# The first pair's down product as seven block products in a second last stage

## The chip, the cores and the metric

The kernel runs on one core of a Trainium2 chip. The metric is device time in microseconds (us) of that core for one launch; the time shown is the median of three runs. Besides the timed runs there is one profiled execution with its trace. Engines: PE (TensorE matmul; its weight loads are listed as PEld), DVE (VectorE), ACT (ScalarE), POOL (GpSimd) and SP (SyncE), which here issues all DMAs.

## The reference

Inputs are float32; S = 2048 tokens, D = 512, F = 1376, 32 heads of 16. The block is a linear attention and a bilinear FFN, each behind a layernorm with a modulation from `c`:

```
mod = silu(c) @ w_mod ; sa, ba, ga, sf, bf, gb = split(mod, 6)
x = A_x + ga * linear_attention(layernorm(A_x) * (1 + sa) + ba)
n = layernorm(x) * (1 + sf) + bf
h = (n @ w_gate) * (n @ w_up)            # 2048 x 1376
out = x + gb * (h @ w_down)              # 2048 x 512
```

The change is in the last line, for half of the tokens and eight elevenths of F. A product of two float32 matrices is made on PE from a high and a low part of each operand (type fp32r): high by high, high by low, low by high, three matmuls for one.

## The kernel before

The tokens are four chunks of 512, each four token tiles of 128; F is eleven f tiles: 0 to 9 of 128 columns and 10 of 96. Chunks 0 and 1 are the first pair, 2 and 3 the second. Attention and the layernorms of the first pair come first. For the first pair f tiles 8, 9 and 10 are done whole, gate, up and down (`gate_up`, lines L958 to L986), beside the attention of the others.

The rest of the FFN is the generator `ffn()`. Its steps each make one f tile's gate and up products for one pair of chunks at once, as a product of 2x2 blocks with seven products in place of eight (`block`; the products are `times`, L1158, 6 matmuls of 512 columns each, 42 a step). The seven follow in the order a11 b11, s1 t1, s2 t2, a12 b21, s3 t3, s4 b22, a22 t4: letters a and s are blocks of the tokens' side and their sums (tile name `h`), b and t blocks of the weights and their differences (tile name `w`). Side work hangs on named points of a step: p1, p5, p6, p2, p7, p3 and p4 stand behind the seven products in that order. The table `plan`, with keys (step, point), and the lists given to `gates` say what is done there. Steps 0 to 7 are the first pair's, with f = 0 to 7; steps 8 to 18 the second pair's.

The weights of a step are a `Right`: four raw loads of 128 KB (L1096), sums on POOL (L1102), high parts on ACT (L1113, L1116), low parts on POOL (L1120). In the first pair's steps the seven tiles of a right are also stored to DRAM (`park`, L1135, seven DMAs of 256 KB), and the second pair's steps fetch them from there (`Fetched`, L1147). The tokens' side of the second pair is made during the first pair's steps; 14 of its tiles are stored (`aside`, L1068) and 14 fetched (`fetch`, L1083) at the end of step 7, since there is no room for both sides. The stows (L1002) are parts of the second pair's normalized tokens on their way through DRAM.

The down product of the first pair is `down_group` (L1241 to L1243). After each second step it takes the two f tiles just made, multiplies their h tiles by rows of w_down (scaled by gb on DVE, split on ACT and POOL), for two chunks of four token tiles, with 24 matmuls of 512 columns at a place (eight such places, cut by `parts` so that they lie between steps), and DVE adds the sums to x (`evac`, L945). So h tiles are used up soon after they are made. The down product of the second pair is the class `Down`: its h tiles stay in the tile pool, five pairs of f tiles (8,9), (0,1), (2,3), (4,5), (6,7) each give 2x2 blocks, tile 10 goes along as an odd one, and after the last step `run` makes seven products, each over the five pairs and partly the odd tile. A product into one pair of PSUM banks uses `mm` (L1455, three matmuls of 256 columns per pair and token tile), one into four banks `mm_wide` (L1463 and L1464, one of 512 and one of 256). The combinations of w_down for it are made during the second pair's steps, stored (L1393) and fetched in the last stage (L1400). The last products' sums are added to x and stored (L1525, L1528).

What sets the order: each engine runs its instructions in program order. All DMAs are issued by SP, in order, and at most eight are outstanding: a DMA waits for the eighth before it. A tile pool of 94 buffers and eight PSUM banks (four named `bank`, four `acc`) limit what can be in flight.

## Time and profile before

| what | value |
|---|---|
| time, median of 3 runs | 540.4 us (539.95 to 540.65) |
| the profiled execution's own time | 539.58 us |
| its span | 537.9 us |
| granted TensorE clock | 1.00 |
| PE busy | 532.6 us, 99% of the span |
| DVE, ACT, POOL busy | 408.1, 297.7, 160.0 us |
| moved by DMA | 109.21 MB, mean 203 GB/s |

The span runs from the first to the last instruction; the time is some 1.7 us more than the span. A busy time is the sum over an engine's instructions without idle time between them. In the trace the first pair's steps run from about 250 to 363 us, the second pair's from 363 to 478.9, and the second pair's down product from there to the end.

### The profile page before, as it was taken

What the parts mean: (1) busy time and instruction counts of PE and PEld (TensorE: products, weight loads), DVE (VectorE), ACT (ScalarE), POOL (GpSimd) and SP (SyncE); (2) the same over time, 40 slices, a digit from 0 to 9 for tenths busy, and PEclk for the clock granted to TensorE, in tenths of its full rate; (3) what the DMA queues carried; (4) which work ended last, traced back from release to release, by engine and by line L of the source; (5) the groups of instructions that cost most, each with busy time, mean ns of one, the idle gap of its engine ahead of it and who ended that gap; (6) DMA issues with size and microseconds to landing.
All of it is one profiled execution on the core that took longest, in us unless ns stands there. A gap on an engine that the chain in (4) does not pass through costs nothing.

```text
span 537.9 us, 8026 instructions
## 1 busy us (share of the span) xinstructions
PE 532.6 (99%) x2549; PEld 444.7 (83%) x2549; DVE 408.1 (76%) x701; ACT 297.7 (55%) x564; POOL 160.0 (30%) x170
## 2 busy tenths in 40 slices
PE   8999999999999999999999999999999999999997
PEld 7888888888888878878888888887888888889997
DVE  7997879999989888779766576996556564669772
ACT  3696877648587765577684545454434334246030
POOL 2001010010021220076696577747532322210000
PEclk9999999999999999999999999999999999999999
DMA  8902427310165165947869596794289998689222
GB/s 283 387 35 92 144 98 216 98 60 2 45 195 194 41 209 147 310 143 228 279 197 319 207 323 224 216 372 120 74 300 334 388 389 315 229 278 392 83 77 81
DMA packets 86396, 109.21 MB, mean 203 GB/s; under 512 B 10897, under 2 KB 41617, under 8 KB 86353
## 3 DMA queue, kind: packets, MB, share of 16 engines
q1 hardware_dynamic: 86352, 108.70, 60.3%
q8 instruction: 20, 0.33, 0.3%
q14 instruction: 24, 0.19, 0.1%
HBM read 65.93 MB, written 42.73 MB: 202 GB/s over the span
## 4 chain that ended last, share of the span: by engine, by line
PE 99%; DVE 0%; issue 0%
PE bank L1158 27%; PE acc L875 8%; PE acc L1158 7%; PE acc L1455 6%; PE bank L209 4%; PE bank L211 4%; PE bank L210 4%; PE bank L1463 3%; PE acc L416 3%; PE acc L418 3%; PE acc L417 3%; PE acc L1242 3%; PE acc L1241 3%; PE acc L1243 3%; PE bank L958 2%; PE bank L960 2%
## 5 line engine op out<-in xcount | busy, mean ns | idle before, releaser
L1158 PE MATMUL bank<-h,w 128*128 128x512 f32 (+1 forms) x630 | 145.4, 389 | 0.0
L1158 PEld LDWEIGHTS bank<-h,w 128*128 128x128 f32 (+1 forms) x630 | 117.0, 186 | 26.1 <-DVE u L1220 0.2
L1163 ACT ACTIVATE bank<-bank 128x512 f32<-128x512 f32 (+1 forms) x30 | 17.5, 583 | 74.0 <-PE bank L1158 73.8
L197 DVE TENSOR_TENSOR kl<-u,kh 128x512 fp32r<-128x512 f32 (+1 forms) x38 | 26.3, 736 | 23.9 <-ACT kh L196 21.9
L265 POOL TENSOR_TENSOR rstd<-ve,half 128x2 f32<-128x2 f32 (+3 forms) x13 | 11.8, 911 | 107.8 <-DVE ve L264 44.5
L209 PE MATMUL bank<-w,h 128*128 128x512 f32 x104 | 40.8, 392 | 0.0
L211 PE MATMUL bank<-w,h 128*128 128x512 f32 x104 | 40.6, 391 | 0.0
L210 PE MATMUL bank<-w,h 128*128 128x512 f32 x104 | 40.5, 390 | 0.0
L1158 PE MATMUL acc<-h,w 128*128 128x512 f32 x168 | 38.7, 389 | 0.0
L197 POOL TENSOR_TENSOR w<-raw,w 128x512 fp32r<-128x512 f32 (+1 forms) x15 | 22.2, 1483 | 53.4 <-ACT w L196 47.8
L875 PE MATMUL acc<-w,xh 128*128 128x512 f32 x120 | 37.1, 390 | 0.0
L1158 PEld LDWEIGHTS acc<-h,w 128*128 128x128 f32 x168 | 31.5, 188 | 6.5
L945 DVE TENSOR_TENSOR x<-acc,x 128x512 f32<-128x512 f32 x40 | 26.5, 686 | 12.8 <-PE acc L1243 11.1
L1120 POOL TENSOR_TENSOR w<-raw,w 128x256 fp32r<-128x256 f32 (+3 forms) x22 | 23.9, 1084 | 37.4 <-ACT w L1113 33.2
L1455 PE MATMUL acc<-w,kh 128*128 128x256 f32 (+1 forms) x176 | 31.8, 283 | 0.0
L1120 POOL TENSOR_TENSOR w<-t,w 128x512 fp32r<-128x512 f32 (+1 forms) x22 | 30.2, 1372 | 0.0
L1455 PEld LDWEIGHTS acc<-w,kh 128*128 128x128 f32 (+1 forms) x176 | 27.5, 192 | 0.2
L875 PEld LDWEIGHTS acc<-w,xh 128*128 128x128 f32 x120 | 22.4, 188 | 4.6
L416 PE MATMUL acc<-kh,xh 128*128 128x512 f32 x64 | 25.2, 394 | 0.0
L418 PE MATMUL acc<-kl,xh 128*128 128x512 f32 x64 | 25.0, 391 | 0.0
L417 PE MATMUL acc<-kh,xl 128*128 128x512 f32 x64 | 25.0, 390 | 0.0
L1241 PE MATMUL acc<-w,kh 128*128 128x512 f32 x64 | 24.9, 389 | 0.0
(258 smaller groups left out, 1325.5 us busy)
## 6 DMA issues: line engine op xcount, KB each, us to landing
right<-w SPq DMA_DIRECT2D x56, 256.0 KB, 3.6
w<-right SPq DMA_DIRECT2D x56, 256.0 KB, 5.1
raw<-in_w_mod_dram SPq DMA_DIRECT2D x24, 256.0 KB, 3.9
raw<-in_B_w_down_dram SPq DMA_DIRECT2D x20, 256.0 KB, 4.2
down_t<-w SPq DMA_DIRECT2D x20, 256.0 KB, 5.1
w<-down_t SPq DMA_DIRECT2D x20, 256.0 KB, 5.4
x<-in_A_x_dram SPq DMA_DIRECT2D x16, 256.0 KB, 5.6
down_b<-w SPq DMA_DIRECT2D x15, 256.0 KB, 5.1
```

The lines of the kernel that those rows point to most:

```text
L197: (low or nc.vector).tensor_tensor(l, src, f32(h), op=ALU.subtract)
L209: nc.tensor.matmul(ps, ah, bh, start=i == 0, stop=False)
L210: nc.tensor.matmul(ps, ah, bl, start=False, stop=False)
L211: nc.tensor.matmul(ps, al, bh, start=False, stop=i == n - 1)
L416: nc.tensor.matmul(tacc[k], xh[:, a:b], kh, start=first, stop=False)
L417: nc.tensor.matmul(tacc[k], xl[:, a:b], kh, start=False, stop=False)
L418: nc.tensor.matmul(tacc[k], xh[:, a:b], kl, start=False, stop=last)
L875: nc.tensor.matmul(yps[i], x, y, start=False, stop=k == KD - 1 and x is al, skip_group_check=True)
L1120: sub = lambda out, x, y: (on or nc.gpsimd).tensor_tensor(out, x, f32(y), op=ALU.subtract)
L1158: mm = lambda x, y, **kw: nc.tensor.matmul(ps, x[:, k], y, skip_group_check=True, **kw)
L1241: nc.tensor.matmul(ps, hh[:, a:b], dh[:n, c:d], start=i == 0, stop=False)
L1455: nc.tensor.matmul(ps, x[:, a:b], y, start=start, stop=False, skip_group_check=True)
```

## The change

`down_group`, the loads of w_down for it, `parts` and its 32 adds are removed. The first pair's eight steps follow each other; from step 3 every second one writes the four `acc` banks (`others`) in place of `bank`. Their h tiles are not split but stored to DRAM as they are (`h_park`, two DMAs of 256 KB an f tile, at point p5 of the next step). The second pair begins with f tile 7, whose right stays in place from step 7 (so 49 right tiles are stored and fetched in place of 56), and its order is 7, 10, 8, 9, 0 to 6. The last pair of the class `Down` is now (7,6). A second object of it, `late_down`, makes the first pair's product with the pairs (0,1), (2,3), (4,5), (7,6) after the second pair's, in the same seven products (4 pairs, no odd tile). It fetches 16 h tiles, 28 combinations of the weights a second time (two groups of the last pair are kept and not stored and fetched for the first object), and the four x tiles of chunk 0, which are now stored during the attention (`x_parked`, after `y_step(9)`). Half of its splits' low parts are on POOL.

```diff
-    def down_group(ch, side, js, outs, ds, last, by_tile=False, end=False):
 ...
-    LATE = (10, 8, 9, *range(8))
-    FIRST_AGAIN = len(steps) + 3
-    steps += [((2, 3), f) for f in LATE]
+    FIRST = tuple(range(8))
+    LATE = (7, 10, 8, 9, *range(7))
+    ODD, LAST = 10, (7, 6)
+    steps = [((0, 1), f) for f in FIRST] + [((2, 3), f) for f in LATE]
+    FIRST_AGAIN = len(steps) - 7
+    KEPT = len(FIRST)
 ...
     def right_load(n):
-        if n < FIRST_AGAIN:
+        if n == KEPT:
+            rights[n] = rights[n - 1]
+        elif n < FIRST_AGAIN:
             rights[n] = Right(steps[n][1])
 ...
-        if free[0] and parts:
-            takes = [down_group(*p) for p in parts.pop(0)]
-            yield
-            for take in takes:
-                take()
+    def h_park(f, out):
+        h_parked[f] = []
+        for n, x in enumerate(out):
+            h_parked[f].append(tc.dram_tile([P, D], F32, name=f"h_{f}_{n}"))
+            nc.sync.dma_start(h_parked[f][n], x)
 ...
+        for m, (cs, f) in enumerate(steps[:KEPT]):
+            out = []
+            more = {"p1": []}
+            if m < KEPT - 1:
+                more["p1"].append(lambda: rights[m].park(f))
+            if m:
+                more["p5"] = [lambda: h_park(*before)]
+            if m == KEPT - 1:
+                more["p1"].insert(0, lambda: fetch(stash, second_side, ("a11", 0), ("a11", 1), ("s1", 0)))
+                more["p7"] = [lambda: fetch(stash, second_side, ("s2", 0), ("a12", 0), ("a12", 1), ("s3", 0))]
+            if m == 2:
+                others.extend(acc_bank() for _ in range(4))
+            yield from gates(m, cs, side, out, more, raw=True, on=others if m > 2 and m % 2 else None)
+            before = f, out
+        pairs = list(zip(LATE[2:-1:2], LATE[3:-1:2])) + [LAST]
+        wide_down = Down((2, 3), pairs, KEPT)
+        late_down = Down((0, 1), pairs[1:], KEPT, wide_down)
 ...
-        wide_down.run()
+        wide_down.run(others[:2], late_down)
+        late_down.run(others[2:])
 ...
+        def h_fetch(self, n, side):
+            for fs in self.fs:
+                self.h.setdefault(fs[n], [None] * 2)[side] = load(h_parked[fs[n]][side], "u")
 ...
-                split(self.a(i, name), h, l)
+                split(self.a(i, name), h, l, nc.gpsimd if self.of and i % 2 else None)
 ...
+            if then:
+                then.h_fetch(0, 0)
+                then.w_fetch("b11")
+                then.h_fetch(0, 1)
+                then.h_fetch(1, 1)
             self.product(A, js, "s4", "b22", False, odd(0, 1))
 ...
+            if then:
+                then.h_fetch(1, 0)
+                then.w_fetch("b21")
+                xts[then.cs[0]] = [load(to, "x") for to in x_parked]
+                then.h_split("a11", *range(then.NI))
+                for i in range(then.NI):
+                    then.h_sum("s1", i)
+                    then.h_sum("s3", i)
 ...
+    x_parked = []
+    for j in range(NJ):
+        x_parked.append(lift_out(f"x_{j}", xts[0][j]))
```

On PE, at the end of the third of the first pair's steps, the kernel before has the last matmuls of that step's last product and then a down group (acc is a group's PSUM bank, kh and kl the split rows of w_down, w here the split h tiles):

```order
L1158 MATMUL bank_2875<-h_2435,w_3117 128x512
L1158 MATMUL bank_2875<-h_2436,w_3117 128x512
L1158 MATMUL bank_2875<-h_2435,w_3124 128x512
L1241 MATMUL acc_3285<-w_3002,kh_3035 128x512
L1242 MATMUL acc_3285<-w_3003,kh_3035 128x512
L1243 MATMUL acc_3285<-w_3002,kl_3036 128x512
```

In the changed kernel the same place on PE reads so:

```order
L1158 MATMUL bank_2883<-h_2435,w_3109 128x512
L1158 MATMUL bank_2883<-h_2436,w_3109 128x512
L1158 MATMUL bank_2883<-h_2435,w_3116 128x512
L1158 MATMUL acc_3163<-h_1961,w_3229 128x512
L1158 MATMUL acc_3163<-h_1962,w_3229 128x512
L1158 MATMUL acc_3163<-h_1961,w_3229 128x512
```

The group has gone and the fourth step's first product stands there at once, in another PSUM bank.

On SP, in that same step, the kernel before parks the last right tile, loads rows of w_down and the raw weights of the step after next, and goes on with the next park:

```order
L1135 DMA right_6_3202<-w_3124 128x512
L113 DMA raw_3236<-in_B_w_down_dram 128x512
L1096 DMA raw_3238<-in_B_w_gate_dram 128x2x128
L1096 DMA raw_3238<-in_B_w_up_dram 128x2x128
L1096 DMA raw_3239<-in_B_w_gate_dram 128x2x128
L1096 DMA raw_3239<-in_B_w_up_dram 128x2x128
L1135 DMA right_0_3332<-w_3244 128x512
```

In the changed kernel the same place on SP reads so:

```order
L1135 DMA right_6_3186<-w_3116 128x512
L1275 DMA h_0_3196<-u_3076 128x512
L1275 DMA h_1_3198<-u_3054 128x512
L1096 DMA raw_3223<-in_B_w_gate_dram 128x2x128
L1096 DMA raw_3223<-in_B_w_up_dram 128x2x128
L1096 DMA raw_3224<-in_B_w_gate_dram 128x2x128
L1096 DMA raw_3224<-in_B_w_up_dram 128x2x128
L1135 DMA right_0_3273<-w_3229 128x512
```

Two stores of h tiles have taken the place of the load of w_down.

On SP, at the end of the first pair's steps, the kernel before has f tile 10's raw loads (that tile comes first in its second pair), and then stores and the first of the fetches:

```order
L1096 DMA raw_3884<-in_B_w_gate_dram 128x2x96
L1096 DMA raw_3884<-in_B_w_up_dram 128x2x96
L1068 DMA side_s_0_0_3920<-h_3916 128x512
L1068 DMA side_s_0_1_3922<-h_3917 128x512
L1083 DMA h_3990<-side_a_0_0_3527 128x512
```

There the changed kernel has the fetches of the second side's tiles between stores, and the last eight of them read so (the last two are s3's):

```order
L1275 DMA h_1_3775<-u_3650 128x512
L1083 DMA h_3805<-side_s_0_0_3723 128x512
L1083 DMA h_3806<-side_s_0_1_3725 128x512
L1083 DMA h_3809<-side_a_0_0_3479 128x512
L1083 DMA h_3810<-side_a_0_1_3481 128x512
L1083 DMA h_3813<-side_a_1_0_3611 128x512
L1083 DMA h_3814<-side_a_1_1_3613 128x512
L1083 DMA h_3817<-side_s_0_0_3679 128x512
L1083 DMA h_3818<-side_s_0_1_3681 128x512
L1096 DMA raw_3821<-in_B_w_gate_dram 128x2x96
```

The fetches stand as they did before with regard to each other; stores of h tiles stand ahead of them, and f tile 10's raw loads have moved from ahead of the fetches to behind them.

More of the change, by code (lines that the diff above doesn't have):

```diff
@@ L1333, in ffn @@
         wide_down.planned()
         for n, f in enumerate(LATE):
+            m = KEPT + n
             out = wide_down.h.setdefault(f, [])
-            if n == 3:
-                others.extend(acc_bank() for _ in range(4))
-            more = {"p1": [lambda: rights.update({m + 1: Fetched(steps[m + 1][1])})]} if FIRST_AGAIN <= m + 1 < len(steps) else {}
-            yield from gates(m, (2, 3), second_side, out, more, raw=f != LATE[0], on=others if n > 2 and n % 2 else None)
-            m += 1
+            more = {}
```

129 lines of the change are left out of this document (48 added, 81 removed).

## The prediction

> **What bounds the kernel now.** I read the page first, then the waits of TensorE, then windows by stage, then the timelines of TensorE and of the SP queue in the stages that the change touches.
>
> ```profile
> span 537.9 us, 8026 instructions
> ...
> PE 532.6 (99%) x2549; PEld 444.7 (83%) x2549; DVE 408.1 (76%) x701; ACT 297.7 (55%) x564; POOL 160.0 (30%) x170
> ...
> PEclk9999999999999999999999999999999999999999
> DMA  8902427310165165947869596794289998689222
> ...
> PE 99%; DVE 0%; issue 0%
> ```
> ```profile
> PE acc L146 <- DVE w L141: 2.0, 1, 2.0
> ```
>
> The reader is to see that PE is busy in 99% of the span, that the granted clock is full in each slice, that the chain which ended last is PE, and that PE's only recorded wait is 2.0 us, early on. So the time is PE's own work: what the change takes off PE comes off the time, and what it lets PE wait is added. The digits of the DMA row say where such a wait could come from: the DMA engines stand at 8 and 9 in several stretches. The next rows give stretches of the span (start, end, length; busy time and count of PE, PEld, DVE, ACT, POOL; granted clock; DMA share; GB/s).
>
> ```profile
> 282.00:345.00 63.00, 63.00 (x279) 52.10 (x278) 43.29 (x65) 32.49 (x61) 41.27 (x40) 1.00 0.75 256
> 350.00:360.00 10.00, 10.00 (x45) 8.04 (x45) 9.58 (x14) 7.48 (x16) 5.88 (x5) 1.00 1.03 390
> 417.00:425.00 8.00, 8.00 (x37) 6.64 (x36) 3.88 (x6) 2.42 (x7) 2.14 (x3) 1.00 1.05 391
> 478.90:537.90 59.00, 55.67 (x401) 52.41 (x399) 41.85 (x84) 14.72 (x26) 0.00 (x0) 1.00 0.48 170
> ```
>
> The first row is most of the first pair's steps, and there the DMA engines already work 0.75 of the time. The next two are stretches in which they are full: 390 and 391 GB/s, thus 262,144 bytes in 0.67 us. PE loses nothing in any of them. In the last row the down product of the second pair has DVE at 41.85 of 59 us.
>
> **PE's work.** The old down product of the first pair is 8 token tiles x 8 f tiles x 3 = 192 matmuls of 512 columns. The new one is 7 products x 4 token tiles x 4 pairs = 112 groups; four products write the narrow way (three matmuls of 256 columns a group, 64 groups), three the wide way (one of 512 and one of 256, 48 groups).
>
> ```profile
> 259.52 23.28 PE L1158 MATMUL bank<-h,w 128*128 128x512 f32 x102
> 282.64 0.39 PE L1241 MATMUL acc<-w,kh 128*128 128x512 f32 x1
> ...
> 303.04 9.72 PE L1158 MATMUL bank<-h,w 128*128 128x512 f32 x42
> ...
> 363.08 9.84 PE L1158 MATMUL bank<-h,w 128*96 128x512 f32 x42
> ...
> 478.86 0.40 PE L1455 MATMUL acc<-w,kh 128*128 128x256 f32 x2
> ...
> 486.05 0.40 PE L1463 MATMUL bank<-w,kh 128*128 128x512 f32 x1
> ...
> 494.48 0.40 PE L1455 MATMUL acc<-w,kh 128*128 128x256 f32 x2
> ```
>
> Durations of single matmuls overlap, so I take starts. From 259.52 to 282.64 stand 102 matmuls of 512 columns: 0.2267 us each, so a step of 42 is 9.52 us and the 192 removed are 43.5 us. From 478.86 to 486.05 stand 20 narrow groups: 0.36 us each, 64 of them 23.0. From 486.05 to 494.48 stand 24 wide groups: 0.351 each, 48 of them 16.9. PE's work falls by 43.5 - 39.9 = 3.6 us. A group has as many columns in either form as these rows, so I give this term no more than 0.3 us either way.
>
> **The first pair's steps lose their cover.** The removed groups lay between the steps and gave every other engine and the SP queue time. Behind the change the third step is followed by the fourth at once. Into the shorter time go the same parks and, besides them, two parks of h tiles a step; what goes out is one load of w_down a step and the park of f tile 7.
>
> ```profile
> 269.71 8.78 SPq L1002 DMA_DIRECT2D stowed<-n  x16
> 278.59 3.83 SPq L1135 DMA_DIRECT2D right<-w  x7
> ...
> 283.20 0.60 SPq L1096 DMA_DIRECT2D raw<-in_B_w_gate_dram  x1
> 283.85 0.57 SPq L1096 DMA_DIRECT2D raw<-in_B_w_up_dram  x1
> 284.51 0.42 SPq L1096 DMA_DIRECT2D raw<-in_B_w_gate_dram  x1
> 284.99 0.46 SPq L1096 DMA_DIRECT2D raw<-in_B_w_up_dram  x1
> ```
> ```profile
> stowed<-n SPq DMA_DIRECT2D x16, 64.0 KB, 1.8
> ```
> ```profile
> 344.80 2.01 SPq L1083 DMA_DIRECT2D h<-side_a  x4
> ...
> 358.15 0.79 SPq L1083 DMA_DIRECT2D h<-side_s  x2
> 359.00 0.42 SPq L113 DMA_DIRECT2D raw<-in_B_w_down_dram  x1
> ```
> ```profile
> h<-side_s SPq DMA_DIRECT2D x6, 256.0 KB, 5.9
> ```
>
> I count transfers from 278.59, the end of the stows: those are small ones that land 1.8 us after their issue, so nothing is piled up behind them, and the third step ends at 282.64 in both kernels, since nothing ahead of it on PE changes. From there to the last tile that the second pair's first step needs of the fetch (s3, the fifth of its seven products), the changed queue holds, in its fixed order: 35 parks of right tiles, 12 parks of h tiles, 4 loads of u, 14 stores and 14 fetches of the second side, which is 79 transfers of 256 KB, and 16 raw loads of 128 KB. The 79 at 0.67 us are 52.9 us. The raw loads were issued 0.42 to 0.60 us apart; by bytes at 391 GB/s they would be 0.34 each: 5.4 to 8.2 us, and I take 7.7, near the issues, since these transfers lie in shorter runs. With some 2 us from the first issue to the first landing the last fetch lands at 278.6 + 52.9 + 7.7 + 2 = 341.2. PE, unhindered, starts the second pair's first step at 282.64 + 5 x 9.52 = 330.2 and its fifth product 24 matmuls later, at 335.7. So it waits **5.5 us**. The kernel before had room there: the same two tiles issued at 358.15 and landing 5.9 later are in at 364.1, and needed at 363.08 + 5.4 = 368.5.
>
> Bounds: at 0.65 us a transfer and 0.34 a raw load the wait is 1.5 us (51.4 + 5.4 + 1.9 from 278.6 is 337.3). The 21 issues from 344.80 to 359.00 stand 0.676 apart; with 0.51 a raw load that is 53.4 + 8.2 + 2, 342.2, and 6.5 us. If parks wait for POOL so that the queue is idle in between, each idle microsecond is added; I allow up to 1.5 more, so 8. I take 5.5.
>
> The second step of the second pair needs f tile 10's raw loads, which stand behind that fetch: they land about 2 us behind it, some 343, and POOL makes the combinations from them.
>
> ```profile
> L1102 POOL TENSOR_TENSOR t<-raw,t 128x256 f32<-128x256 f32 x16 | 12.9, 805 | 0.6
> L1120 POOL TENSOR_TENSOR w<-raw,w 128x256 fp32r<-128x256 f32 x10 | 8.2, 816 | 33.2 <-ACT w L1113 33.2
> L1120 POOL TENSOR_TENSOR w<-raw,w 128x512 fp32r<-128x512 f32 x10 | 13.9, 1386 | 0.0
> L1120 POOL TENSOR_TENSOR w<-t,w 128x512 fp32r<-128x512 f32 x20 | 27.7, 1385 | 0.0
> ```
>
> A step's right costs POOL four sums and four lows: 4 x 0.805 + 0.816 + 1.386 + 2 x 1.385 = 8.2 us, against 9.52 of PE. It fits, with 1.3 us of room that was 6 and more with a group of 24 matmuls (5.4 us) beside each step. The raw loads come late in steps 4, 6 and 7, after stores and parks; I expect waits of up to 1 us there. They do not add: the SP queue's order runs on meanwhile, so PE arrives later at the same late fetch. For f tile 10 I add 0.3. The h parks themselves cost PE nothing, only the queue. The 32 adds on DVE, one scale a step and POOL's split of each w_down tile fall away here; none of them held PE, so nothing is gained by that.
>
> **The last stage.** Here 39.9 us of PE work stand at the end, with 16 fetches of h, the weights' combinations once more (28) and four x tiles on the queue.
>
> ```profile
> 480.16 9.68 SPq L1400 DMA_DIRECT2D w<-down_t  x15
> 515.64 19.75 SPq L1528 DMA_DIRECT2D out_dram<-x  x12
> ```
> ```profile
> 481.15 3.10 DVE L197 TENSOR_TENSOR kl<-u,kh 128x512 fp32r<-128x512 f32 x5
> 484.16 1.29 DVE L1417 TENSOR_TENSOR u<-s,u 128x512 f32<-128x512 f32 x2
> ...
> 507.59 3.23 DVE L1525 TENSOR_TENSOR x<-x,bank 128x256 f32<-128x256 f32 x8
> ...
> 534.61 0.42 DVE L1525 TENSOR_TENSOR x<-x,acc 128x256 f32<-128x256 f32 x1 [1.73 <-PE acc L1455]
> ```
>
> Fetches there issue 0.645 us apart (15 in 9.68). The first h fetch stands behind the first four of the stores that begin at 515.64 and goes at about 519 on the old clock; the first product needs 4 h tiles and 4 of b11 besides, in by about 526, when the old stage still has 8 us to run: hidden. The third product's t2 tiles stand 36 transfers behind the first fetch (16 of h, b11, b21, x, out stores and t2): 519 + 36 x 0.67 + 2 = 545, and the third product starts at 534.4 + 23 x 0.5 = 545.9: just in time. DVE has 28 sums and differences or lows of 0.6 and 32 adds of 0.4 there, with some splits given to POOL; 42 us over all against 40 of PE, with a part done ahead. Bounds: 0 where all of it hides, 2 us where each of the first three products waits for the queue. I add **0.2**. The tail behind the last matmul stays: one add of 0.42 us and a store.
>
> **The early part.** Four stores of x stand ahead of the first raw loads: 4 x 0.67 = 2.7 us later at most, at a place where the DMA digits are 1 to 6. I cost it at nothing; if that cover fails, it is 2.7 less the slack, at most 1.
>
> **Sum.** -3.6 + 5.5 + 0.3 + 0.2 = +2.4 us. The profiled execution took 539.58 us as timed, 0.8 below the median of 540.4; it would become 542.0, and the median **542.8**. Some 0.2%, or 1.1 us, is what a measurement of this kernel can tell from no change.
>
> The sum stands on the queue's price for a transfer, and the Trainium skill has a page on it: "DMA: Bandwidth & Descriptors", sections Specifications and Bandwidth, gives about 358 GB/s as a core's limit against HBM, and 435 as the ceiling of the fabric. By 358 a transfer would be 0.73 us, and the wait 4.9 us longer: about 547.5. By 435 it would be 0.60, and the wait would be nearly gone. The trace has 390 and 391 over 8 and 10 us, and the trace decides.
>
> **Rivals.**
> (a) The queue keeps up, and the change is faster. The mechanism: parks and fetches move at 0.60 us or less, so the s3 fetch lands at 278.6 + 79 x 0.60 + 16 x 0.34 + 2 = 333.4, ahead of 335.7. The point from which it decides is 0.63 us a transfer. For it: the 7 parks at 278.59 were issued in 3.83 us, 0.55 each. Against it: eight may be outstanding, so a first burst issues faster than it moves, and the full stretches say 0.67. It gives 540.4 - 3.6 = 536.8.
> (b) Half of the wait is there, because part of the stores and fetches move where I took the queue as full: a wait of 2.6 to 4.7 us with all small terms, and a time within 1.1 us of 540.4, about 540.4.
> (c) POOL becomes the bound of the first pair's steps: rows of 0.74 to 1.05 us for a sum and lows up to 1.8 occur, and 10 us a step over five steps is 2.5 us; since the fetch waits behind it on the queue (parks wait for POOL's lows), the two add: about 545. Against it: 8.2 us by the means.
> (d) The last stage starves on the queue and on DVE, 2 to 3 us: also about 545.
>
> A wait in one piece may cost twice. The granted clock in this trace is full throughout, so no row shows what a pause of some microseconds does. The Trainium skill, "TensorE: Matmul & The Clock Gate", Part 1, says that an idle window of about 3.4 us halves the clock until about 3.4 us of work have passed. By that, if the wait came in one piece, 1.7 us would be added, 544.5; my wait comes in pieces of 3 us (the step's first product, whose tile a11 lands 12 transfers ahead of the last) and less, and I leave the sum.
>
> **How the numbers follow.** My forecast, the wait of 4 to 8 us: 0.43, with 541.0 to 545.5 as its own range. (a) 0.23. (b) 0.18. (c) and (d) together 0.16. Faster by over 0.2% is (a), 0.23; the same is (b) and the low edge of the forecast, 0.18; slower is the rest, 0.59. Cases of both signs are needed for eight in ten, so the range goes from (a), 536.8, to the dear end of the slow ones, 547.5.
>
> **What would show it.** In the profile after: PE's busy time about 3.6 us lower; PE's waits name the second pair's first step (h by DMA, L1083's tiles), some 5 us in sum between products one and five; the DMA share above 0.95 from the fourth step to that place; POOL busy over 8 us a step without PE waiting for it by more than 1 us; in the last stage PE without waits above 1 us. I would be wrong if PE had no wait there, which says that a transfer is cheaper than 0.63 us or that the order leaves the queue fewer of them, or if the largest wait were at another place.

## The result and the profile after

The changed kernel takes 566.2 us (median of 4 runs, 562.6 to 568.0) against 540.2 us of the kernel before: 1.0475 times as long, with a 95% interval of 1.0451 to 1.0499. Forecast were 542.8 us and a range of 536.8 to 547.5. The direction is as forecast, the size more than ten times too small (26.0 us in place of 2.4). The profiled execution of the changed kernel took 562.61 us, 3.6 below its median, with a span of 560.9 against 537.9. The 23.0 us between the two spans are what follows; the other three executions took 565.7 to 568.0 us at a granted clock of 0.981 to 0.985 in place of 0.988, and where their further 3 to 5 us lie is not shown.

From the page after, the rows that answer to those shown of before:

```profile
span 560.9 us, 8341 instructions
...
PE 536.4 (96%) x2645; PEld 447.6 (80%) x2645; DVE 411.5 (73%) x719; ACT 302.9 (54%) x568; POOL 159.8 (28%) x172
...
PEclk9999999999999999999999999997999999997999
DMA  8903346400354268767799999139987797279913
...
PE 81%; DMA 8%; POOL 4%; issue 2%; DVE 2%; SPq 2%; ACT 1%; POOLq 0%; ACTq 0%; DVEq 0%
```

PE's share fell from 99% to 96%, though its busy time did not fall by 3.6 us as forecast but rose by 3.8: a busy time also grows where matmuls run at half clock or stand apart for less than a listed wait. The clock shows a 7 in two slices where it had 9 throughout, and the chain that ended last is no longer PE alone: 8% of it is DMA and 4% POOL. The longest of PE's waits after (engine, line, what it waited for: us in total, times, the longest):

```profile
PE acc L1158 <- ACT acc L1163: 8.5, 2, 6.4
PE acc L1429 <- DVE x L1508: 6.3, 1, 6.3
PE acc L146 <- DVE w L141: 2.0, 1, 2.0
PE bank L1158 <- DMA h<-side_s: 1.9, 1, 1.9
```

Only the last row is at the place of the forecast wait. The timeline of PE tells where the time is (start, length, what; the idle time ahead and who ended it). The steps change between `acc` and `bank`, so their starts can be read:

```profile
282.62 9.68 PE L1158 MATMUL acc<-h,w 128*128 128x512 f32 x42
...
335.62 3.86 PE L1158 MATMUL bank<-h,w 128*128 128x512 f32 x12
...
341.38 3.12 PE L1158 MATMUL bank<-h,w 128*128 128x512 f32 x10 [1.90 <-DMA h<-side_s]
...
349.93 2.23 PE L1158 MATMUL acc<-h,w 128*96 128x512 f32 x9
...
369.48 5.61 PE L1158 MATMUL acc<-h,w 128*128 128x512 f32 x24
...
381.46 5.95 PE L1158 MATMUL acc<-h,w 128*128 128x512 f32 x18 [6.37 <-ACT acc L1163]
...
387.25 1.98 PE L1158 MATMUL bank<-h,w 128*128 128x512 f32 x8
...
453.89 0.40 PE L1429 MATMUL acc<-w,kh 128*128 128x256 f32 x2
...
511.58 0.79 PE L1429 MATMUL acc<-w,kh 128*128 128x256 f32 x2 [6.30 <-DVE x L1508]
...
557.06 0.28 PE L1429 MATMUL acc<-w,kl 128*128 128x256 f32 x1
```

A step is 9.52 us of PE. I call step 3 the one that starts at 282.62; step 8 is the second pair's first (f tile 7), step 9 f tile 10, step 11 f tile 9.

| stretch | from, to | length | PE's own work | lost |
|---|---|---|---|---|
| steps 3 to 8 | 282.6, 349.9 | 67.3 | 57.1 | 10.2 |
| steps 9 and 10 | 349.9, 369.5 | 19.6 | 19.2 | 0.4 |
| step 11 | 369.5, 387.25 | 17.75 | 9.5 | 8.2 |
| steps 12 to 18 | 387.25, 453.9 | 66.6 | 66.6 | 0 |
| last stage | 453.9, 557.34 | 103.4 | 55.7 + 39.9 | 7.8 |

Lost are 26.6 us, and PE's work is 3.6 less than before: 23.0, which is the difference of the spans. So there are three places, and the table of the step starts, read so for each run below, is the measure of the experiments.

The last stage also bears out the work that was forecast for it. In the chain of waits the late product's narrow products stand as whole pieces (16 groups of three each), with a wide one from 534.6 to 540.2:

```profile
528.87 5.76 PE acc L1429 x48
...
540.19 5.75 PE acc L1429 x48
```

Four of 5.76 and three of 5.56 to 5.66 are 39.9 us, as forecast.

**Place 1, steps 3 to 8.** Windows of after (columns as in the prediction's):

```profile
282.60:340.00 57.40, 52.93 (x223) 40.85 (x221) 36.20 (x50) 33.01 (x59) 33.13 (x33) 1.00 1.01 353
```

The DMA engines are busy throughout, but at 353 GB/s and not at the 391 of the prediction's windows: 0.74 us for 262,144 bytes. In forty slices of this window the rate is not even (GB/s):

```profile
GB/s 375 383 279 202 400 401 401 382 255 200 347 355 393 403 397 397 380 294 343 395 394 391 380 385 294 237 383 395 394 393 393 388 384 368 244 361 267 297 410 387
```

Runs of stores go at some 380 to 403, near the 391 of the prediction; the dips stand where raw loads are on the queue and, from 331 us, where the fetches follow the stores. Why the rate falls there is not shown. The fetch of the last s3 tile, on which the forecast wait hangs, is in the chain of waits (issue, us to landing):

```profile
333.65 6.98 DMA h<-u
...
340.70 5.23 DMA h<-side_s
```

It lands at 345.9. An unhindered PE would need it 5 x 9.52 + 5.44 us after the start of step 3, at 335.7: it is 10.2 us late, and 10.2 us are what steps 3 to 8 lose. Part of that, 5.4 us, is lost ahead of step 8, in waits for DVE, POOL and ACT in steps 4, 6 and 7, and 4.8 in step 8, where PE meets the late tiles one by one: 12 matmuls from 335.62 take 3.86 us in place of 2.72. These losses do not add to the lateness of the fetch; they are parts of it.

**Place 2, step 11.** POOL's timeline shows 18 us of idleness until f tile 10's raw loads land; from there it works with hardly a pause until 376.5. SP's timeline and DVE's show who waits:

```profile
346.68 0.59 POOL L1102 TENSOR_TENSOR t<-raw 128x192 f32<-128x192 f32 x1 [18.11 <-DMA raw<-in_B_w_up_dram]
...
373.73 2.79 POOL L1329 TENSOR_TENSOR w<-t,w 128x256 fp32r<-128x256 f32 x4
```
```profile
367.96 6.15 SPq L1360 DMA_DIRECT2D down_b<-w  x3
374.49 0.32 SPq L1360 DMA_DIRECT2D down_t<-w  x1
374.90 0.90 SPq L113 DMA_DIRECT2D raw<-in_B_w_down_dram  x2
```
```profile
377.82 0.69 DVE L1337 TENSOR_TENSOR raw<-raw,row 128x512 f32<-128x512 f32 x1 [7.45 <-DMA raw<-in_B_w_down_dram]
```
```profile
379.99 0.42 ACT L1328 ACTIVATE w<-raw 96x256 fp32r<-96x256 f32 x1 [6.92 <-DVE raw L1416]
```

SP wants to store four of the down product's weight combinations (L1360), which POOL has not made; behind them stand two loads of w_down; DVE waits 7.45 us for these at its scale (L1337); behind the scale on DVE stands the odd tile's difference (L1416), ACT waits for that, and behind ACT's split stands the PSUM copy (L1163) that PE needs. In the kernel before, POOL has pauses there, ahead of a right's lows and ahead of the combinations:

```profile
382.61 0.77 POOL L1120 TENSOR_TENSOR w<-raw,w 128x256 fp32r<-128x256 f32 x1 [4.50 <-ACT w L1113]
...
393.06 1.44 POOL L1362 TENSOR_TENSOR w<-raw,w 128x256 fp32r<-128x256 f32 x2 [4.53 <-ACT w L1361]
```

**Place 3, the last stage.** The chain of waits at 500 us:

```profile
499.58 5.50 DMA u<-h
...
505.15 4.60 DMA out_dram<-x
...
509.78 0.69 DVE s L1391
...
510.50 0.69 DVE u L1391
511.19 0.34 DVE x L1508
...
511.58 3.48 PE acc L1429 x16
```
```profile
505.79 0.69 DVE L1391 TENSOR_TENSOR s<-u,u 128x512 f32<-128x512 f32 x1 [2.69 <-DMA u<-h]
```

DVE stands 2.69 us idle for a fetch of h tiles, and from 505.79 its eight sums for the late product (L1391) take 5.3 us. (The chain goes by way of an output store that landed at 509.75; DVE has no idle time there.) The sums stand in DVE's order ahead of the adds (L1508) that read a PSUM bank of the product before, into which PE is to write next. So a product that needs nothing of the late product waits 6.3 us for that product's fetches and sums.

### The profile page after: what moved, and what is told of

Same layout as the page of the kernel before. It is cut to its first block, busy times and chain, and to the rows that moved or that the text cites. A ratio compares the mean times of both kernels' runs of the same rounds, so it can differ in the third digit from the quotient of the medians.

```text
span 560.9 us, 8341 instructions
## 1 busy us (share of the span) xinstructions
PE 536.4 (96%) x2645; PEld 447.6 (80%) x2645; DVE 411.5 (73%) x719; ACT 302.9 (54%) x568; POOL 159.8 (28%) x172
## 4 chain that ended last, share of the span: by engine, by line
PE 81%; DMA 8%; POOL 4%; issue 2%; DVE 2%; SPq 2%; ACT 1%; POOLq 0%; ACTq 0%; DVEq 0%
PE bank L1158 12%; PE acc L1429 9%; PE acc L875 7%; PE acc L1158 7%; PE bank L1437 5%; PE bank L211 4%; PE bank L209 4%; PE bank L210 4%; PE acc L416 3%; PE acc L418 3%; PE acc L417 3%; PE bank L1438 2%; PE bank L958 2%; PE bank L960 2%; PE bank L959 2%
## 5 line engine op out<-in xcount | busy, mean ns | idle before, releaser
L1158 PE MATMUL bank<-h,w 128*128 128x512 f32 x462 | 110.0, 393 | 4.1 <-DMA h<-side_s 1.9
L1158 PEld LDWEIGHTS bank<-h,w 128*128 128x128 f32 x462 | 85.9, 188 | 26.5 <-ACT h L196 2.3
L1158 PE MATMUL acc<-h,w 128*128 128x512 f32 (+1 forms) x336 | 80.1, 396 | 8.6 <-ACT acc L1163 8.5
L1158 PEld LDWEIGHTS acc<-h,w 128*128 128x128 f32 (+1 forms) x336 | 62.9, 188 | 24.5 <-ACT acc L1163 9.3
L1429 PE MATMUL acc<-w,kh 128*128 128x256 f32 (+1 forms) x304 | 56.4, 287 | 6.3 <-DVE x L1508 6.3
L1429 PE MATMUL acc<-w,kl 128*128 128x256 f32 (+1 forms) x152 | 43.5, 286 | 0.0
L1437 PE MATMUL bank<-w,kh 128*128 128x512 f32 x116 | 41.0, 396 | 0.0
L1405 ACT ACTIVATE kh<-u 128x512 fp32r<-128x512 f32 x18 | 11.3, 633 | 43.6 <-DVE u L1391 43.0
L1438 PE MATMUL bank<-w,kl 128*128 128x256 f32 x116 | 32.5, 280 | 0.0
L196 ACT ACTIVATE kh<-u 128x512 fp32r<-128x512 f32 (+1 forms) x38 | 21.8, 621 | 19.1 <-DMA u<-h 17.2
L197 POOL TENSOR_TENSOR kl<-u,kh 128x512 fp32r<-128x512 f32 x8 | 11.2, 1416 | 72.1 <-PE bank L1438 46.7
L1120 POOL TENSOR_TENSOR w<-t,w 128x512 fp32r<-128x512 f32 (+1 forms) x22 | 29.8, 1356 | 0.0
L1163 ACT ACTIVATE bank<-bank 128x512 f32<-128x512 f32 x22 | 12.8, 582 | 31.4 <-PE bank L1158 31.4
L1429 PEld LDWEIGHTS acc<-w,kl 128*128 128x128 f32 (+1 forms) x152 | 29.6, 195 | 0.0
```

Source lines behind the costliest of these rows:

```text
L196: nc.scalar.activation(h, src, AF.Copy)
L197: (low or nc.vector).tensor_tensor(l, src, f32(h), op=ALU.subtract)
L1120: sub = lambda out, x, y: (on or nc.gpsimd).tensor_tensor(out, x, f32(y), op=ALU.subtract)
L1158: mm = lambda x, y, **kw: nc.tensor.matmul(ps, x[:, k], y, skip_group_check=True, **kw)
L1429: nc.tensor.matmul(ps, x[:, a:b], y, start=start, stop=False, skip_group_check=True)
L1437: nc.tensor.matmul(bs[j], h[:, a:b], w[:k].rearrange("p t c -> p (t c)"), start=start, stop=False, skip_group_check=True)
```

## The experiments

Times are medians of four runs; the step lengths are those of one profiled execution each. "Lost" is counted as in the table above. The kernel before, run beside them, had medians of 539.6 to 539.9. Executions of one of these kernels lie up to 5.6 us apart, and kernels that are alike up to step 8 lose 10.2 to 11.7 us in steps 3 to 8, so a difference of 1.5 us in a column says little. In the three kernels with f tiles 5 and 6 made twice another 1.0 us is lost in the last step.

| kernel | time | lost in steps 3 to 8 | in step 11 | in the last stage |
|---|---|---|---|---|
| the change | 566.2 | 10.2 | 8.2 | 7.8 |
| few h stores | 556.9 | 1.2 | 9.1 | 8.4 |
| raw loads ahead | 565.4 | 13.9 | 0.6 (step 10: 6.5) | 8.1 |
| sums behind | 560.8 | 10.7 | 7.8 | 4.4 |
| raw ahead, sums behind, 5 and 6 twice | 559.6 | 12.0 | 8.8 | 4.5 |
| w_down loads ahead | 561.4 | 11.3 | 4.0 | 8.5 |
| two orders | 557.8 | 11.2 | 3.9 | 8.5 |
| two orders, few h stores | 549.75 | 2.1 | 2.3 | 8.2 |
| two orders, 5 and 6 twice | 556.8 | 8.1 | 2.4 | 8.0 |
| half h stores | 561.7 | 7.7 | 9.9 | 7.6 |
| two orders, sums behind | 555.7 | 11.7 | 1.6 | 4.4 |
| two orders, sums on POOL | 559.5 | 11.7 | 1.7 | 9.0 |
| the same, 5 and 6 twice | 557.0 | 7.0 | 2.4 | 9.8 |
| h stores on ACT | 565.6 | 16.6 | 6.9 | 9.8 |
| two DMAs for each h store | 571.1 | 17.9 | 8.4 | 8.7 |
| h stores on ACT, two orders, sums behind | 557.4 | 12.3 | 1.7 | 4.5 |

**Few h stores.**

```diff
     def h_park(f, out):
+        if f:
+            h_parked[f] = h_parked[0]
+            return
```

> Edit: only f tile 0's h tiles are stored, and every late fetch of h reads those (so the late product works on the wrong h tiles); 14 stores of 256 KB fall away, 12 of them between the stows and the fetch of s3. Queue theory: in the changed kernel the DMA engines are full from the fourth step of the first pair to the second pair's first step (share 1.02 and 1.00 at 357 and 344 GB/s, so 0.73 to 0.76 us a transfer), PE is 10.6 us late by the end of that step, and its later wait of 6.4 us in the step of f tile 9 follows from the same lateness by way of f tile 10's raw loads and POOL. Then 12 x 0.73 = 8.8 us of the lateness go, the later wait (8.6 us with the halved clock behind it) goes too, and the time is 548 to 551. Rival 1, POOL is the bound of these steps, with or without the stores: 563 to 566. Rival 2, the place of f tile 10's raw loads behind the fetch makes the later wait, whatever the bytes: 8.8 us go and the later wait stays, 556 to 558.

Measured 556.9, 1.0326 times before (1.0301 to 1.0351). 9.0 of the 10.2 us in steps 3 to 8 go, as the queue theory has it. The wait in step 11 stays, at 5.96 us. The chain of waits of this run there:

```profile
360.55 4.48 POOL w L1120 x4
365.03 1.40 POOL w L1332 x2
366.44 0.32 SPq L1363
...
366.86 0.40 SPq L113
...
367.35 3.03 DMA raw<-in_B_w_down_dram
...
371.09 0.43 DVE raw L1419
...
371.86 0.61 ACT kh L196
372.47 0.49 ACT acc L1163
...
373.00 1.22 PE acc L1158 x2
```

POOL's four lows of a right (L1120), then two of the combinations, then SP's store and the loads behind it, then DVE, ACT and PE. With steps 3 to 8 almost free of waits the same chain is there: place 2 is not the lateness of place 1. My queue theory fell in that half, and rival 2 (556 to 558) had the time.

**Raw loads ahead.**

```diff
-        elif n < FIRST_AGAIN:
+        elif n < FIRST_AGAIN and n not in rights:
 ...
             if m == KEPT - 1:
+                more["p1"].insert(0, lambda: right_load(KEPT + 1))
-                more["p1"].insert(0, lambda: fetch(...
+                more["p1"].insert(1, lambda: fetch(...
```

> Edit: f tile 10's four raw loads are issued ahead of the fetches of step 7 in place of behind them. In the changed kernel POOL stands idle for 18 us until they land at 346.7, and then works off three rights and the w_down parts without a pause until 376.5, while SP's stores of those parts wait for it, the next w_down loads wait behind the stores, DVE waits for the loads, ACT for DVE, and PE for ACT. Theory: POOL starts some 12 us sooner and the wait of 6.4 us with its halved clock (8.6 us) goes; the fetches come 2 us later and PE waits 2 us more at the second pair's first step: 559 to 561. Rival: that later wait comes from the bytes on the queue, whatever POOL does: no gain, 566 to 569.

Measured 565.4, 1.0481 (1.0459 to 1.0502): level with the change. Step 11 lost its wait, but step 10 got one of 4.9 us for a DVE instruction, and steps 3 to 8 lost 3.7 us more. The wait in step 10 is not the loop over SP: ahead of that instruction two of DVE's differences of w_down rows, which take 1.84 us together in the changed kernel, take 6.19, while POOL works without a pause:

```profile
369.50 6.19 DVE L1352 TENSOR_TENSOR t<-raw,t 128x256 f32<-128x256 f32 x2
```

**Sums behind.**

```diff
                 then.h_split("a11", *range(then.NI))
-                for i in range(then.NI):
-                    then.h_sum("s1", i)
-                    then.h_sum("s3", i)
 ...
             add(c1, 0, C, before, (0, HALF))
+            for i in range(then.NI if then else 0):
+                then.h_sum("s1", i)
+                then.h_sum("s3", i)
```

> Edit: DVE's eight sums s1 and s3 of the late product stand behind the last adds of the product before it, in place of ahead of all of them. In the changed kernel these sums wait for the last h fetch (landing at 505.1) and take 5.3 us, and the adds that free the PSUM bank for the turned product stand behind them, so PE waits 6.3 us and then runs at half clock for some 3. Theory: both go, 556 to 558, and PE has no wait above 1 us behind 460 us. Rival: the fetches are late, and the wait shows up again at the late product's third product, which needs the s1: 562 to 566.

Measured 560.8, 1.0386 (1.037 to 1.0401). The 6.3 us are gone, and 3.4 of the 7.8 us of place 3 with them. A new wait, of 2.1 us and again for DVE, stands at the late product's second product, and a half clock behind it. The theory held on the cause; the time lies between the two.

**Raw ahead, sums behind, 5 and 6 made twice.** The edit is the two above, and in `right_load`, `right_sums`, `right_split`, `park` and `Fetched` the steps of f tiles 5 and 6 count as raw ones.

> Edit: the two before this together, and f tiles 5 and 6 are made again from their raw weights in the second pair (their 14 right tiles are neither stored nor fetched; 8 raw loads, POOL's 8.2 us each and ACT's parts come in the last steps instead). Queue theory: 14 x 0.73 = 10.2 us of queue time go ahead of the fetch; of the lateness of 10.6 us plus 2 for the raw loads put ahead, some 2.5 stay, the wait in the step of f tile 9 and the one in the last stage go: 539 to 542, the first kernel with the late product that is level with the one before. Rival 1: POOL is late in the last two steps, with a wait of 3 to 6 us there: 543 to 546. Rival 2: the lateness isn't the queue's: 549 to 552.

Measured 559.6, 1.035 (1.0322 to 1.0379). Rival 2 is nearest, and none of the three came in. 14 stores fewer make steps 3 to 8 only 1.9 us shorter than with the raw loads ahead alone (12.0 against 13.9).

**W_down loads ahead.**

```diff
-                put(a - 1, "p4", lambda i=i: self.w_load(i))
+                put(a - 1, "p3" if i == 1 else "p4", lambda i=i: self.w_load(i))
```

> Edit: the two loads of w_down for the second pair of the class Down are issued two points earlier, ahead of the four stores of the first pair's combinations that wait for POOL; nothing else. The run without most h stores kept its wait of 6.0 us in the step of f tile 9, so that wait isn't the queue's lateness. Theory: the change lets the second pair begin with a right that is kept, so the last right to be made from raw weights (f tile 9) falls one step later with regard to the plan of the class Down and POOL makes its lows ahead of the combinations; SP's stores wait for those, the loads of w_down wait behind the stores, DVE (7.4 us idle) for the loads, ACT for DVE, PE for ACT. With the loads ahead of the stores the wait of 6.4 us and the 1.7 us of half clock behind it go: 557.5 to 559. Rival: POOL itself is the bound there, and PE waits for its lows or for the next right fetched behind the stores instead: 562 to 566.

Measured 561.4, 1.0392 (1.0374 to 1.0411). The wait in step 11 falls from 6.4 to 2.05 us and the step loses 4.0 in place of 8.2, so the order on SP makes half of it (of the 4.0 left, some 1.7 are half clock behind the wait). What is left is on DVE: the loads are in time, but the two scales, of 0.69 us each elsewhere, take 4.47 here, again while POOL works without a pause (that POOL is what slows DVE is not shown by a run of its own):

```profile
372.52 4.47 DVE L1337 TENSOR_TENSOR raw<-raw,row 128x512 f32<-128x512 f32 x2
```

**Two orders.** The edit above, and the eight sums in the late product's `run`, behind its `h_split("a12")`.

> Edit: the loads ahead, and DVE's eight sums of the late product behind that product's first splits and so behind all adds of the product before. Theory: the three losses are separate and add. 6.4 + 1.7 and 6.3 + 1.6 us go: 549.5 to 551.5, with PE's waits in the last stage below 1 us. Rival: one wait hides another (a late stage that starts sooner finds its fetches later): 554 to 557.

Measured 557.8, 1.0343 (1.0314 to 1.0372). The sums at this place cost the last stage as much as they did (8.5): the third product waits 3.5 us for DVE, where the sums now stand ahead of what it needs.

**Two orders, few h stores.** The last edit and the first.

> Edit: both orders, and only f tile 0's h tiles stored, as in the first run (the late product works on the wrong h tiles). If the three losses are all, this is the PE work alone: 540.0 - 3.6 = 536.4 and a few small waits, 537 to 540, below the kernel before. Rival: something else that the late product brings costs PE: 542 or more.

Measured 549.75, 1.0189 (1.0174 to 1.0204): not below the kernel before. Steps 3 to 8 and step 11 still lose some 4.4 us; the last stage keeps 8.2, with the wait of 3.4 us for DVE's and ACT's work, two smaller ones, and the half clock behind them. The rival came in, and it is the last stage.

**Two orders, 5 and 6 twice.**

> Edit: both orders, all h tiles stored, and f tiles 5 and 6 made again from their raw weights in the second pair (14 stores and 14 fetches of 256 KB less). Queue theory: the lateness up to the second pair's first step, some 10 us in the changed kernel, falls to the waits for the second side's stores, 3 to 5 us: 543 to 546. Rival: the lateness isn't in the bytes but in the order of the stores, and stays: 549 to 551.

Measured 556.8, 1.0315 (1.029 to 1.034). Steps 3 to 8 lose 8.1 against 11.2 in the like kernel: the 14 stores are worth 3.1 us there, a third of the 10 that their queue time comes to. The medians are only 1.0 us apart. In the window from 282.60 to 340.00 the DMA share is 0.90 at 306 GB/s in this run, so the queue is no longer full: with fewer transfers something else holds the stores and fetches back. The rival's 549 to 551 is just as far off; the last stage was in neither sum.

**Half h stores.**

```diff
+        if f:
+            h_parked[f] = h_parked[0]
+            for n, x in enumerate(out):
+                nc.sync.dma_start(tc.dram_tile([P, D // 2], F32, ...), x[:, :D // 2])
+            return
```

> Edit: as the first run (late fetches read f tile 0's h tiles, so the late product works on the wrong ones), but the stores of the other h tiles stay, with half of their columns: as many DMAs at the same places, half of the bytes. The first run took 8.4 of the 10.1 us out of the steps from the fourth of the first pair to the first of the second. If the bytes hold these steps, half of that, 4 us, goes: 561 to 563. If it is the number of DMAs and their waits on SP (eight outstanding, in order), nothing goes there: 565 to 567. If the stores matter only as holders of the u buffers until they are done, most goes: 558 to 560.

Measured 561.7, 1.0411 (1.0392 to 1.043). By time this is the bytes' forecast: 4.5 us went, half of the 9.3 of the first run. By the steps it is not: 2.5 us of the 9.0 went from steps 3 to 8, about a quarter, and step 11 lost 1.7 more. The two profiled executions are only 1.1 us apart, since the change's was the shortest of its four; so whether half the bytes give back a quarter or a half is not settled.

**Two orders, sums behind.** The w_down loads ahead, and the sums behind the last adds.

> Edit: the loads of w_down ahead of the four stores, and the eight sums behind the last adds (as in the third run; the kernel with both orders before had them behind the late product's first splits, where PE waited 3.5 us for what DVE makes from the sums). Theory: the gains measured for one edit each, 4.8 and 5.4 us, add: 555 to 557. Rival: they share something: 558 or more.

Measured 555.7, 1.0304 (1.0288 to 1.032). The two gains add, as forecast (4.8 and 5.4, together 10.5 us). It is the best of the kernels that compute all of the reference, and still 16 us behind the kernel before.

**Two orders, sums on POOL,** with the sums behind the first splits:

```diff
-        def h_sum(self, name, *pairs):
+        def h_sum(self, name, *pairs, on=None):
 ...
-                nc.vector.tensor_tensor(to, x, y, op=alu)
+                (on or nc.vector).tensor_tensor(to, x, y, op=alu)
 ...
             for i in pairs if self.of else ():
                 self.h_sum("s1", i)
-                self.h_sum("s3", i)
+                self.h_sum("s3", i, on=nc.gpsimd)
```

> Edit: both orders with the sums behind the first splits, and the four s3 sums on POOL, which is nearly idle in the last stage. Theory: DVE is what the late product's third product waited for (8 sums of 0.61 us ahead of the s2 differences); 2.5 us less on DVE take 2.5 to 5 us off the 557.8 (the half clock behind that wait goes too): 552.5 to 555.5. Rival: POOL's sums take 1.4 us each and s2 has to wait for them: 557 to 560.

Measured 559.5, 1.0378 (1.0347 to 1.0409). PE's wait for DVE is gone, and another is in its place, for a fetch. From PE's waits in this run:

```profile
PE acc L1429 <- DMA w<-down_t: 5.2, 1, 5.2
```

The third product's t2 tiles had been forecast as just in time; with DVE out of the way they are 5.2 us late. The time is the rival's, but the wait is not the one that it named. From 500 to 530 us of this run the DMA share is 0.99 at 360 GB/s and DVE is busy for 22.3 of 30 us, so taking work from DVE leaves the fetches.

**The same, 5 and 6 twice.**

> Edit: the one before, with f tiles 5 and 6 made again in the second pair (14 stores and fetches less). Theory: 556.8 of the like kernel without POOL's sums, less 2.5 to 5: 551.5 to 554.5; still above the kernel before, since the second side's stores and sums keep the first pair's last steps at 10 to 12 us. Rival as before: 556 to 559.

Measured 557.0, 1.032 (1.0296 to 1.0344), in the rival's range. Steps 3 to 8 lose 7.0, the last stage 9.8, with the same wait for the fetch.

**H stores on ACT.**

```diff
-            nc.sync.dma_start(h_parked[f][n], x)
+            nc.scalar.dma_start(h_parked[f][n], x)
```

> Edit: the stores of h tiles are issued by ACT and not by SP; all bytes are moved, nothing else changes. If the bytes hold the steps (DMA engines full), the 10 us stay: 564 to 567. If SP's order and its eight outstanding DMAs hold them (raw loads and fetches behind the stores), most of the 8.9 us that the first run saved go: 557 to 560.

Measured 565.6, 1.0504 (1.0461 to 1.0546). No gain; steps 3 to 8 lose 16.6 (in a profiled execution that took 570.49, 4.9 above the median). But it isn't a clean test: PE's waits for ACT's PSUM copies (L1163) rose from 8.5 us in two waits to 10.3 in three, the first one, of 3.5 us, in step 3, where there was none. There the copy stands behind two of the stores in ACT's order, and these had to wait until 291.68 for a store of a right tile to land: stores in ACT's order hold ACT.

**Two DMAs for each h store.**

```diff
-            nc.sync.dma_start(h_parked[f][n], x)
+            nc.sync.dma_start(h_parked[f][n][:P // 2], x[:P // 2])
+            nc.sync.dma_start(h_parked[f][n][P // 2:], x[P // 2:])
```

> Edit: each h tile is stored by two DMAs of 64 partitions in place of one of 128, all on SP: the same bytes in the same row length, 16 DMAs more. If the bytes hold the steps: 565 to 568. If the number of DMAs does: each pays again what it paid, up to 8.9 us more, 570 to 575.

Measured 571.1, 1.0586 (1.0567 to 1.0606): 4.9 us more than the change, 7.7 more in steps 3 to 8, for the same bytes of h tiles. The window of this run:

```profile
282.60:340.00 57.40, 51.10 (x204) 39.91 (x204) 32.88 (x43) 30.87 (x56) 34.27 (x34) 0.94 0.97 325
```

The DMA engines are as busy as before and move less, 325 GB/s in place of 353. So with the bytes kept the form of the stores counts: twice as many DMAs, each over 64 partitions in place of 128. Whether their number or their width does it, no run tells; and it doesn't show that either counts for more than the bytes.

**H stores on ACT, two orders, sums behind.**

> Edit: the stores of h tiles on ACT, with the loads of w_down ahead of the four stores and the eight sums behind the last adds. By bytes: the 555.7 of the kernel with the two orders, 554 to 557. By SP's order: 547 to 550, still above the kernel before.

Measured 557.4, 1.0348 (1.0311 to 1.0384): the time lies just above what was said for the bytes, and 1.7 us above the like kernel with the stores on SP, which the two intervals do not tell apart. As in the other run with stores on ACT, step 3 is hit: it loses 5.7 of the 12.3 us, where with the stores on SP it loses nothing. So the forecast for SP's order isn't tested cleanly here either.

What the runs do show of steps 3 to 8 is the way of the loss: in each kernel with its h stores on SP the loss equals, within 0.4 us, what the fetch of the last s3 tile is late against an unhindered PE. By its landing in each trace, it is 10.2 us late in the change (lost: 10.2), 1.2 with few h stores (1.2), 7.7 with half of them (7.7), 8.1 with both orders and 5 and 6 twice (8.1) and 17.9 with two DMAs for each (17.9).

What stays open: why the h stores make it so late. Bytes and the number or form of the DMAs both count; whether the latter act through the eight outstanding DMAs, a fixed cost of each DMA, or buffers held until a store is done, these runs do not tell. That 14 stores of another kind (the rights 5 and 6) save a third of their queue time, with the DMA share at 0.90, says that something else stands close behind; DVE's and ACT's side work for the second pair in shorter steps is a guess.

## Why the prediction was wrong

**PE's work, -3.6.** Right: 39.9 us measured for the new product, as forecast, and PE's steps of 9.52 with no loss where nothing waits (steps 12 to 18). The sign named for it failed: PE's busy time rose by 3.8 us. Half clock adds 3.2 us to it, and matmuls that stand apart, as the 12 at 335.62, add more, so the busy time does not measure the work here.

**The wait at the second pair's first step, 5.5 (up to 8).** Right in kind, mis-sized: what steps 3 to 8 lose, 10.2 us, is the lateness of the s3 fetch, which landed at 345.9 and not at 341.2. The step that failed is the price of 0.67 us a transfer. It came from windows that fetches fill; over this stretch the mean was 0.74, which for the 79 transfers is 5.5 us more. The row that would have said so stood in the prediction: 256 GB/s at a share of 0.75 in the first pair's own steps is 341 GB/s at a full share, 0.77 us. I took the price from the wrong stretch. By the slices of the rate, runs of stores kept near the price; the mean is pulled down at the raw loads and from 331 us on, where fetches follow stores. "They do not add", of the waits ahead of that step, held: PE came to step 8 at 335.62 and not at 330.2, 5.4 us late, and lost 4.8 more inside it, and the two together are the 10.2 of the fetch.

The Trainium skill, "DMA: Bandwidth & Descriptors", section Bandwidth, gives about 358 GB/s as what a core has against HBM. The means after lie near it (353 in steps 3 to 8, 363 from 500 to 530 us), and I had set the rule aside with the 391 of another stretch. The trace does not show it as a limit: inside steps 3 to 8 slices stand at 390 to 403. With the prediction's estimate by that figure, 4.9 us more, the sum would have been 547.7, still far below 566.2: the other places weigh more than the price.

**0.3 for f tile 10's step, and POOL that "fits".** Place 2, 8.2 us in step 11, is missing from the sum. The sum over a step, 8.2 of 9.52 us, was right and beside the point: it left out POOL's work for the class `Down`, which in the kernel before had pauses of 4.5 us around it. With the kept right of f tile 7 in front, the last right to be made from raw weights falls one step later, just ahead of the first combinations that SP waits for. I followed the queue of each engine, but not the loop through SP's order: a store that waits for POOL holds a load for DVE. The run with w_down's loads ahead of the stores shows half of it (8.2 to 4.0 us); the run with few h stores shows that it is no echo of the late fetch.

**0.2 for the last stage.** It lost 7.8: the wait of 6.3 and the half clock behind it. I had weighed DVE's total (42 of 40 us) and the landing of fetches, and both as averages. What failed is the order: sums that wait for a fetch stand ahead of adds that free a PSUM bank. The later runs show that the averages are no comfort either: with DVE's order and part of DVE's load changed, the next wait is the fetch of t2, 5.2 us.

**The clock.** I left 1.7 us out of the sum since my wait came in pieces. The waits of 6.4 and 6.3 us came in one piece, and behind them PE ran at half clock until 384.9 and 514.6, for 3.4 and 3.0 us:

```profile
378.00:384.00 6.00, 2.54 (x6) 2.08 (x7) 2.34 (x4) 2.84 (x7) 2.42 (x4) 0.50 0.89 315
508.00:514.00 6.00, 2.42 (x11) 2.42 (x12) 3.79 (x7) 1.89 (x3) 0.61 (x1) 0.50 1.05 378
```

These cost 1.7 and 1.5 us, 3.2 of the 26.6 lost. Here the Trainium skill, "TensorE: Matmul & The Clock Gate", Part 1, agrees with the trace: half clock until some 3.4 us of work have passed.

**The rivals.** (d), a starved last stage, came at three times its price (7.8 us against 2 to 3), and together with the forecast wait, where I had it as an alternative. (c) did not come as put: in the first pair's steps PE waited 0.6 us for POOL. What came is a wait with POOL in its loop in another step, through SP's order, at three times (c)'s 2.5 us. (a) is refuted: a transfer took 0.74 us on the mean, not 0.60. And the sign that I had named against the whole held: the largest waits, 6.4 and 6.3 us, stand at other places than the second pair's first step.

## What to carry to other kernels

When covering work is taken out of a stage, every in-order queue in that stage is a suspect: look for an instruction that waits for another engine and has behind it one that a third engine needs, and price that loop, not the engines' totals. Take the price of a transfer from the stage in question, as rate over share, and not from the stretch with the best rate. Where several mechanisms each have a condition that is only just not met, they may all come at once; treat them as terms of one sum and not as rivals.

## What the runs showed of the hardware

A wait need not be long to cost clock. In the run with the w_down loads ahead a wait of 2.05 us was followed by 3.5 us at a granted clock of 0.51, while a wait of 2.10 us in the changed kernel, in its step 7, had none behind it (its granted clock first falls at 378.0 us). The first row is of the changed kernel, the other two of the run with the loads ahead:

```profile
331.38 4.40 PE L1158 MATMUL acc<-h,w 128*128 128x512 f32 x18 [2.10 <-ACT acc L1163]
```
```profile
379.36 5.99 PE L1158 MATMUL acc<-h,w 128*128 128x512 f32 x18 [2.05 <-ACT acc L1163]
```
```profile
380.50:384.00 3.50, 3.50 (x10) 2.72 (x9) 2.67 (x4) 0.66 (x2) 3.50 (x5) 0.51 0.89 282
```

And with the h tiles stored by twice as many DMAs, each over half of the partitions, the same stretch of the clock moved 325 in place of 353 GB/s with the DMA engines as busy as before (0.97 and 1.01); it does not hold quite the same transfers, since that run is behind. Inside the changed kernel's stretch the rate goes from 200 to 410 GB/s between slices, and the DMA share is 0.8 or more in each: a full DMA share doesn't say how much is moved.
